# Holding the first four attention chunks to their order of emission, and moving the first weight conversions behind them

## The chip, the cores and the metric

The kernel runs on one core of a Trainium2 chip. The metric is the device time of one execution in microseconds; lower is better. Each comparison ran the kernel before on the same chip in the same rounds. All executions quoted are of the state "fast"; inside that state single executions of one kernel differ by up to 3.3 us (once 5.4 us), and part of this study is about why.

## The reference

The first half is linear attention with a decaying state, for 4 batches, 8 heads, 768 steps and head size 48. The second half is a gated feed-forward network over the 3072 resulting rows of width 384.

```python
f = 1.0 / (1.0 + np.exp(-f_logit))
for t in range(S):
    state = f[:, :, t, :, None] * state + np.einsum('bhd,bhe->bhde', k[:, :, t], v[:, :, t])
    y[:, :, t] = np.einsum('bhd,bhde->bhe', q[:, :, t], state)
...
g = x @ w_gate                     # 384 x 1536
silu = g * (1.0 / (1.0 + np.exp(-g)))
return (silu * (x @ w_val)) @ w_out
```

The weights arrive as 64-bit floats. The kernel turns them into 32-bit floats itself, in 18 pieces of 768 KB.

## The kernel before

The sequence is cut into chunks of 128 steps; a chunk of one batch is one unit of attention (the prediction and the expectations call a unit a chunk). The four units of the first 128 steps (one per batch) come first. From then on the feed-forward matmuls of one group of 128 steps alternate with the attention of the next group. Six steps make up a unit:

```python
def attention(u):                                   # steps 0 to 5, cut
    p = transposed("fTp", fr)                       # TensorE               step 0
    nc.scalar.activation(gate..., p, AF.Sigmoid)    # ScalarE
    yield
    nc.vector.tensor_tensor_scan(tail, gate, ...)   # VectorE, and three small operations   step 1
    yield
    kp = transposed("kTp", kr); qp = transposed("qTp", qr)                # step 2
    nc.vector.tensor_tensor(kT, kp, tail...)        # VectorE
    nc.vector.tensor_tensor_scan(head, gate, start, ...)
    nc.vector.tensor_tensor(qT, qp, head...)
    yield
    # sc <- kT, qT (TensorE); A <- sc * causal (VectorE, two halves); kt       step 3
    yield
    # y <- A, v (TensorE); x <- y (ScalarE); dS <- kt, v; state <- dS          step 4
    yield
    # xTp <- x (TensorE); xT <- xTp (ScalarE)                                  step 5
```

A weight piece takes three calls: a fetch (DMA), `sizes` (two ScalarE operations, `up` and `top`, of some 0.9 us each) and `join` (four VectorE operations, some 3 us together). The order in which the kernel emits all this for the first four units:

```python
for u in range(NRAW): load(u)         # f, k, q, v of three units
keep_warm(5)                          # 5 matmuls of zeros, for the clock of TensorE
...
run(0, 0, 1, 2); load_after(0)
for _ in range(3): fetches.pop(0)()   # three weight pieces
for b in range(1, B):
    if b == 1:
        run(1, 0)
        keep_warm(12)                 # 12 more, in the gap before the first sc
    run(b, 1); run(b - 1, 3); run(b, 2)
    if b + 1 < B:
        run(b + 1, 0)
    else:
        for _ in range(2): sizes.pop(0)()
    run(b - 1, 4)
    if b > 1:
        run(b - 2, 5); load_after(b - 1)
run(B - 1, 3); joins.pop(0)()
run(B - 1, 4); run(B - 2, 5); run(B - 1, 5)
joins.pop(0)(); load_after(B - 1)
```

Emission is not the final order. A scheduler reorders each engine's instructions by its own estimate of when they will be ready. In the build of before it put all 17 warm-up matmuls first, the second unit's scan ahead of the first unit's `kT`, and operations of three weight pieces ahead of the fourth unit's `A`.

## Time and profile before

| | before |
|---|---|
| time, median of the first three executions | 741.44 us |
| span of the profiled execution | 740.4 us |
| first transpose (fTp) / second fTp | 7.39 / 8.70 us |
| first sc / fourth sc | 14.22 / 34.10 us |
| fourth unit's y / first gate matmul | 38.63 / 44.62 us |

The prediction below shows the page, the timeline of TensorE and the chain. In addition, this is the table of windows of the kernel before, in stretches of 10 us: the window and its length, then for each engine the busy time and the number of instructions (matmul, weight load, VectorE, ScalarE, GpSimd), then the granted clock of TensorE, the DMA share and GB/s.

```profile
10.00:20.00 10.00, 5.78 (x35) 5.58 (x35) 7.95 (x15) 0.59 (x2) 0.00 (x0) 0.66 1.02 227
...
30.00:40.00 10.00, 7.30 (x84) 6.11 (x83) 8.37 (x14) 4.93 (x10) 0.00 (x0) 1.00 0.88 200
40.00:50.00 10.00, 9.83 (x33) 6.42 (x33) 4.68 (x8) 4.22 (x8) 0.83 (x1) 0.66 0.44 114
```

Two kinds of loss are to be told apart here. In the first and second line TensorE has too few busy microseconds; in the first and third its clock is 0.66, so a busy microsecond is worth less. The third line looks almost full (9.83) and still loses some 3.3 us (34% of 9.83). A stretch at half clock is called a cold spell below.

### The profile page before, as it was taken

Reading aid. Unit: us, or ns where it says so; the run is one execution under the profiler, and the core shown is the slowest. Engines: PE = TensorE matmul, PEld = TensorE weight load, DVE = VectorE, ACT = ScalarE, POOL = GpSimd, SP = SyncE. Lnnn points to the kernel's source line nnn. Section 1 sums busy time; section 2 is a strip of 40 time slices with the busy share of each in tenths; the row PEclk is TensorE's granted clock in tenths of the full one; section 3 lists DMA queues with packets and bytes.
Section 4 is the critical chain, followed back from the end, with each engine's and each line's share of the span. In section 5 each row is a group of like instructions: output and inputs, shape, how many; then the busy total and the mean of one; then the engine's idle time right before and its main releaser. Section 6 shows DMA issues by size and latency. Waiting matters only on the chain.

```text
span 740.4 us, 7631 instructions
## 1 busy us (share of the span) xinstructions
PE 725.4 (98%) x3146; PEld 420.9 (57%) x3146; DVE 248.5 (34%) x405; ACT 185.0 (25%) x272; POOL 21.0 (3%) x43
## 2 busy tenths in 40 slices
PE   6999999999999999999999999999999999999997
PEld 4855555665565565555566556556555555544454
DVE  6859679303343102423400334310333230011100
ACT  1644566103323012231301322301223120111100
POOL 2000000000000000000000000000000000000000
PEclk8989999999999999999999999999999999999999
DMA  9947556012211101211200121110100000000000
GB/s 185 242 149 190 157 165 171 12 32 43 43 21 33 39 26 34 43 32 33 43 21 23 43 43 22 33 32 22 27 18 1 0 1 22 23 0 1 0 23 24
DMA packets 109772, 38.34 MB, mean 52 GB/s; under 512 B 100512, under 2 KB 103584, under 8 KB 109728
## 3 DMA queue, kind: packets, MB, share of 16 engines
q1 hardware_dynamic: 106272, 33.04, 18.9%
q10 hardware_dynamic: 3456, 4.72, 1.8%
q8 instruction: 27, 0.44, 0.2%
q14 instruction: 17, 0.14, 0.1%
HBM read 33.03 MB, written 4.72 MB: 51 GB/s over the span
## 4 chain that ended last, share of the span: by engine, by line
PE 95%; DVE 3%; ACT 1%; issue 0%; ACTq 0%; DVEq 0%
PE gate L564 25%; PE o L580 25%; PE val L564 25%; PE y L519 5%; PE sc L499 3%; PE y L516 3%; PE kt L506 1%; PE dS L526 1%; PE kTp L462 1%; PE qTp L462 1%; PE fTp L462 1%; PE idle L340 1%; PE xTp L542 1%; DVE tails L472 0%; DVE head L485 0%
## 5 line engine op out<-in xcount | busy, mean ns | idle before, releaser
L564 PE MATMUL gate<-xT,w_gate 128*128 128x512 f32 x432 | 197.7, 599 | 0.8 <-ACT xT L543 0.5
L564 PE MATMUL val<-xT,w_val 128*128 128x512 f32 x432 | 195.7, 595 | 0.1
L580 PE MATMUL o<-w_out,h 128*128 128x384 f32 x576 | 188.8, 487 | 0.0
L580 PEld LDWEIGHTS o<-w_out,h 128*128 128x128 f32 x576 | 108.4, 190 | 73.0 <-issue 0.5
L564 PEld LDWEIGHTS val<-xT,w_val 128*128 128x128 f32 x432 | 79.2, 190 | 86.4 <-issue 85.3
L564 PEld LDWEIGHTS gate<-xT,w_gate 128*128 128x128 f32 x432 | 79.2, 192 | 85.1 <-issue 82.5
L575 DVE TENSOR_TENSOR h<-h,val 128x512 f32<-128x512 f32 x72 | 49.3, 685 | 185.7 <-PE val L564 185.7
L571 ACT ACTIVATE h<-gate 128x512 f32<-128x512 f32 x72 | 43.0, 597 | 208.7 <-PE gate L564 208.5
L472 DVE TENSOR_TENSOR_SCAN tails<-gates,ones 128x516 f32<-128x516 f32 x24 | 29.6, 1233 | 100.2 <-ACT gates L467 100.1
L501 DVE TENSOR_TENSOR A<-sc,causal 128x512 f32<-128x512 f32 x48 | 30.9, 684 | 79.8 <-PE sc L499 79.8
L583 ACT COPY ob<-o 128x384 f32<-128x384 f32 x24 | 11.5, 478 | 183.5 <-PE o L580 183.5
L519 PE MATMUL y<-v,A 128*128 128x48 f32 x384 | 54.4, 270 | 2.7 <-DVE A L501 2.4
L519 PEld LDWEIGHTS y<-v,A 128*128 128x128 f32 x384 | 50.7, 196 | 3.2 <-DVE A L501 2.7
L499 PEld LDWEIGHTS sc<-qT,kT 48*128 48x128 f32 x384 | 24.7, 193 | 20.1 <-issue 17.5
L499 PE MATMUL sc<-qT,kT 48*128 48x128 f32 x384 | 29.7, 292 | 4.9 <-DVE qT L487 4.9
L485 DVE TENSOR_TENSOR_SCAN head<-gates,starts 128x516 f32<-128x516 f32 x24 | 33.7, 1406 | 0.7
L491 POOL TENSOR_TENSOR decayed<-state,tails 128x384 f32<-128x384 f32 x20 | 16.8, 840 | 574.9 <-DVE tails L472 574.9
L516 PE MATMUL y<-decayed,qT 128*128 128x96 f32 x160 | 32.7, 286 | 0.0
L516 PEld LDWEIGHTS y<-decayed,qT 128*128 128x128 f32 x160 | 25.8, 192 | 8.5 <-issue 6.9
L467 ACT ACT_TABLE_LOAD x20 | 25.7, 1283 | 16.1 <-PE fTp L462 13.5
L532 DVE TENSOR_TENSOR state<-decayed,dS 64x192 f32<-64x192 f32 x32 | 11.2, 351 | 48.1 <-PE dS L526 47.9
L571 ACT ACT_TABLE_LOAD x20 | 25.7, 1283 | 0.4
(58 smaller groups left out, 356.1 us busy)
## 6 DMA issues: line engine op xcount, KB each, us to landing
fraw<-in_f_logit_dram SPq DMA_DIRECT2D x24, 192.0 KB, 2.8
kraw<-in_k_dram SPq DMA_DIRECT2D x24, 192.0 KB, 2.7
qraw<-in_q_dram SPq DMA_DIRECT2D x24, 192.0 KB, 3.3
v<-in_v_dram SPq DMA_DIRECT2D x24, 192.0 KB, 3.5
w<-in_moe_w_gate_dram SPq DMA_DIRECT2D x6, 768.0 KB, 5.5
w<-in_moe_w_val_dram SPq DMA_DIRECT2D x6, 768.0 KB, 5.4
w<-in_moe_w_out_dram SPq DMA_DIRECT2D x6, 768.0 KB, 4.3
out_dram<-ob ACTq DMA_DIRECT2D x24, 192.0 KB, 1.8
```

Source lines behind the costliest of these rows:

```text
L462: nc.tensor.transpose(p[:, a * C:(a + 1) * C], src[:, 2 * a:2 * a + 2, :].rearrange("t r d -> t (r d)"), ident)
L467: nc.scalar.activation(pairs(gate)[:, :, 1:N1], p, AF.Sigmoid)
L472: nc.vector.tensor_tensor_scan(tail[:, 0:n][:, ::-1], gate[:, 0:n][:, ::-1], ones[:, ::-1], 1.0, op0=ALU.mult, op1=ALU.add)
L485: nc.vector.tensor_tensor_scan(head, gate[:, 0:n], start, 1.0, op0=ALU.mult, op1=ALU.add)
L499: nc.tensor.matmul(sc[par][:, a * C:(a + 1) * C], lhsT=kT[r, a, :], rhs=qT[r, a, :], start=True, stop=True)
L501: nc.vector.tensor_tensor(A[:, par], sc[par].rearrange("p (a t) -> p a t", t=C), causal.unsqueeze(1).broadcast_to((128, HP, C)), ALU.mult)
L516: nc.tensor.matmul(both, lhsT=qT[:, a, :], rhs=decayed[:, a, :, :].rearrange("p r d -> p (r d)"), start=True, stop=False, skip_group_check ...
L519: nc.tensor.matmul(both[:, par * D:(par + 1) * D], lhsT=A[:, par, a, :], rhs=vt[u][:, 2 * a + par, :], start=(c == 0), stop=True, skip_gro ...
L564: nc.tensor.matmul(p, lhsT=w[:, i, j * 128:(j + 1) * 128], rhs=xT[c][:, i, :], start=(i == 0), stop=(i == KT - 1))
L571: nc.scalar.activation(h[j], p, AF.Silu)
L575: nc.vector.tensor_tensor(h[j], h[j], p, ALU.mult)
L580: nc.tensor.matmul(p, lhsT=h[j][:, b * C:(b + 1) * C], rhs=w_out[:, j, :], start=(j == 0), stop=(j == NF - 1))
```

## The change

Its intent is that TensorE, VectorE and ScalarE run the first four units exactly as emitted: every instruction emitted since a mark gets an order edge (no semaphore, only an order) to the one before it on its engine. The second piece's `sizes` are emitted last, so that they do not stand in ScalarE's way.

```diff
     for u in range(NRAW):
         load(u)
+    traced = nc.cur_bb.bb.instructions
+    mark = traced[-1]
     keep_warm(5)
...
+    def in_order(since):
+        start = next(i for i, ins in enumerate(traced) if ins is since) + 1
+        for engine in (mybir.EngineType.PE, mybir.EngineType.DVE, mybir.EngineType.Activation):
+            mine = [ins for ins in traced[start:] if ins.engine == engine]
+            for a, b in zip(mine, mine[1:]):
+                tc.add_manual_dep(b, a.name, mybir.DependencyInfo(mybir.DependencyClass.NoSync,
+                                                                  mybir.DependencyReason.DATA), reason="order")
...
         else:
-            for _ in range(2):
-                sizes.pop(0)()
+            sizes.pop(0)()
...
     run(B - 1, 5)
+    sizes.pop(0)()
     joins.pop(0)()
     load_after(B - 1)
+    in_order(mark)
```

## The prediction

> **What bounds the kernel now.** I read the page's busy shares and slices first, then the table of windows, then the timeline of TensorE up to 75 us, then the chain of waits through the one hole that is left.
>
> ```profile
> PE 725.4 (98%) x3146; PEld 420.9 (57%) x3146; DVE 248.5 (34%) x405; ACT 185.0 (25%) x272; POOL 21.0 (3%) x43
> ...
> PE   6999999999999999999999999999999999999997
> ...
> PEclk8989999999999999999999999999999999999999
> ```
>
> TensorE is busy for 98% of 740.4 us. Only the first three slices (18.5 us each) show anything else: idle time in the first and third, a lowered clock in the first and third. From about 47 us on TensorE runs without a gap at full clock, so the end is "start of the feed-forward matmuls plus a fixed amount of TensorE work". The change touches only what is before that start: the attention of the first four chunks. In the timeline of TensorE the lines that count are:
>
> ```profile
> 1.25 6.30 PE L340 MATMUL idle<-blank 128*128 128x512 bf16 x17 [1.25 <-DVE blank L335]
> 7.39 0.60 PE L462 MATMUL fTp<-ident,fraw 128*128 128x128 f32 x4
> ...
> 8.70 0.60 PE L462 MATMUL fTp<-ident,fraw 128*128 128x128 f32 x4
> 14.22 2.08 PE L499 MATMUL sc<-qT,kT 48*128 48x128 f32 x16 [4.92 <-DVE qT L487]
> ...
> 38.63 0.42 PE L519 MATMUL y<-v,A 128*128 128x48 f32 x2 [2.41 <-DVE A L501]
> ...
> 44.62 6.62 PE L564 MATMUL gate<-xT,w_gate 128*128 128x512 f32 x12
> ```
>
> All 17 warm-up matmuls run at the very start and delay the first transpose to 7.39, although its data was there at 3.5 (issue at 0.80 plus 2.7 us to landing in the DMA view of that issue). Then TensorE stands idle 4.92 us for VectorE, later 2.41 us more. Each hole brings a cold spell, as the windows show (last three columns: clock, DMA share, GB/s):
>
> ```profile
> 13.50:16.20 2.70, 1.98 (x16) 1.82 (x16) 1.81 (x2) 0.00 (x0) 0.00 (x0) 0.50 1.05 210
> 16.20:19.90 3.70, 3.70 (x20) 3.67 (x18) 2.67 (x4) 0.58 (x1) 0.00 (x0) 0.50 0.99 258
> ...
> 40.50:44.00 3.50, 3.33 (x17) 2.93 (x17) 0.97 (x2) 1.08 (x3) 0.00 (x0) 0.50 0.00 1
> 44.00:47.20 3.20, 3.20 (x8) 1.65 (x7) 1.82 (x5) 2.16 (x3) 0.53 (x1) 0.50 0.50 100
> ```
>
> The second hole comes from conversions of weights that the scheduler put ahead of the last chunk's masking (A). The chain shows it:
>
> ```profile
> 35.73 0.80 ACT top L410
> 36.53 0.02 issue
> 36.55 0.04 DVE top L416
> 36.59 0.44 issue
> 37.03 0.95 DVE top L419
> 37.98 0.61 DVE A L501
> 38.59 0.04 issue
> 38.63 0.42 PE y L519 x2
> ```
>
> VectorE waits for ScalarE's pass over the third weight piece (the timeline gives that wait 1.60 us), and A, whose scores were ready, stands behind it.
>
> **What the Trainium skill says.** "TensorE: Matmul & The Clock Gate", Part 1, says the array runs at half clock until a free-running window of about 3.4 us was busy, and falls back after an idle one. The trace agrees on the size (0.50, two spells of some 6.8 us) and on the cause. By the spacing of the warm-up matmuls, 11 to 12 start in the first 4.3 to 5 us (0.4 us each) and 6 in the last 1.3 us (0.22 us), so the clock came up about 6.2 us after the start, though the page prints full clock there. The same page, in the part on PE-mode transpose, says that transposes do not count as busy for the gate; here the clock came back at 19.9 us after 3.7 us in which TensorE did nothing but transposes, so this trace does not bear it out. Part 1 also says that VectorE and ScalarE take instructions strictly in order, which is what the chain shows at 36.55. "DMA: Bandwidth & Descriptors", Specifications, asks for 512 B or more per descriptor for full rate: the attention loads go in runs of 192 B at about 200 GB/s with a DMA share near 1, the weights' stretch at 18 to 22 us at about 400. So the early loads are bound by the DMA, not by who waits for them, and their landings should stay where they are.
>
> **The change part by part.** By the order of instructions in the two builds:
> 1. Only 5 warm-up matmuls stay at the start. 12 follow the second chunk's fTp, so they lie in the old 4.92 us hole.
> 2. VectorE does each chunk's own chain in turn: the second chunk's scan (1.23 us) no longer precedes the first chunk's qT, and no weight conversion precedes the fourth A.
> 3. The first join follows the fourth A; the second and third pieces' conversions come after the last xT copy.
> 4. From the gate matmuls on the order is nearly as before; five more transposes of chunk five (0.11 us each, 0.55 us) are done before the gate instead of after.
>
> New start S of the first sc: two paths meet. Through VectorE: 5 cold warm-ups end at 3.4; fTp from 3.55, cold, takes 1.06 (as the rows at 17 to 19 us before), to 4.6; sigmoid 0.60, to 5.25; scan 1.23, to 6.5; the three small ones 0.54 (21.85 to 22.39 before); kT 0.6, head 1.15, qT 0.7 with small gaps, to 9.6. Through TensorE: the second chunk's f lands at 7.36 (3.76 + 3.6), fTp to 7.9, 12 warm-ups at 0.216 = 2.6 us, to 10.5. So S = 10.5 if the clock is up by 7.5, instead of 14.22: the warm-ups now cost 0.8 us. If the clock comes up one window later S is about 12; if two, about 13.2.
>
> From S to the first gate, with the warm starts of the rows at 22 to 36 us: sc 1.09, kt 0.49, kTp 0.48, qTp 0.48, fTp 0.44, y 1.81, dS 0.60, xTp 0.48. Chunk 1 without xTp is 5.39, chunk 2 with all 5.87, chunk 3 without fTp 5.43, so the fourth sc is at S + 16.7. It and kt take it to S + 18.3; A ends at S + 18.55 (two of 0.6 us after the second half of sc), so y starts at S + 18.6; y 1.8, dS 0.6, xTp 0.8, fTp 0.45, kTp 0.45, half of qTp 0.2 give S + 22.9. The gate's xT copy ends at about S + 22.7, the first join 2.9 us after A (S + 21.5). VectorE needs 5.4 us a chunk (scan 1.23, small ones 0.54, A 1.2, kT 0.6, head 1.2, qT 0.65), under TensorE's 5.4 to 5.9, so TensorE stays the bound, by 0.5 to 0.7 us.
>
> First gate: 10.5 + 22.9 = 33.4. Before, it was 44.62, and the clock was half until 47.2, which costs (47.2 - 44.62) / 2 = 1.3, so 45.9 in warm time. Saved: 45.9 - 33.4 = 12.5, plus the 0.55 of transposes done earlier = 13.1 us. With the clock one window late 11.6, two late 10.3.
>
> After the gate: w_val's first piece is the tight one. ScalarE starts on it at S + 22.7 and does it and the next one (1.7 us each), VectorE's join follows the other piece's first operation, and ends about 0.4 us before the first val (gate + 5.15). Later pieces land 8 to 18 us after the new gate start, each some 5 us before its matmul. I count nothing for them.
>
> **The rivals.** (a) The warm-ups inside the order become a toll: cold, they cost 0.43 each, 5.1 us, on the path to sc. For it: TensorE idles from 6.35 to 7.4 for the second f, and transposes may count for less. Against: before, the same first five microseconds sufficed. It leaves 10 to 11 us: 731. (b) The weights become the bound, since conversions start later and TensorE asks 12 us earlier. For: the 0.4 us margin, DMA share near 1 until 40 us. Against: only two pieces are needed in the first 10 us and they land by 22.7. It would give back 1 to 4 us: 730 to 733. (c) The strict order itself adds waits, with four PSUM banks turning round; the margins I find are 0.25 to 0.8 us. If VectorE becomes the bound, 0.5 us a chunk: 1 to 2 us. (d) Everything hidden because TensorE has the work to do anyway: no; the saved time is idle time and half clock, which nothing else fills.
>
> **Range and chances.** The best I can build is S = 9.7: 13.9 us saved, 727.5. The middle of the clock cases (6 in 10 early, 3 one window late, 1 two late) is 12.3 us: 741.44 - 12.3 = 729.1; a little friction makes 729.5. Two per cent would need 726.6, which is below my best case, so faster by over 2% takes an error of mine of about 1 us in the favourable direction: 0.1. Within 2%: 0.89. Slower: 0.01. Range 726.8 to 733.5.
>
> **What would show it.** First transpose near 3.6; sc at 10 to 12 with no idle of 4.9 us before it; clock full from about 13 to the end without the 0.50 spells; no wait of y for A above 0.5 us; first gate at 33 to 36; feed-forward busy time per matmul unchanged. I am wrong if the gate starts after 38, if TensorE shows new idle time at val or gate for w_val or w_gate, or if a cold spell lies among the warm-ups or later.

## The result, and the profile after

The changed kernel took 730.33 us (median of 4, 729.28 to 731.38) against 741.32 us for the kernel before. The ratio is 0.9849, with a 95% interval of 0.9829 to 0.9869. Ratios here are the mean time of one kernel's fast runs over that of the other's of the same rounds, so they are not quite the ratio of the medians quoted. That it is faster is beyond doubt, since the interval lies below 1.

The page of the changed kernel, the same lines as before (busy share, busy tenths and clock in 40 slices of 18.2 us):

```profile
PE 718.8 (99%) x3146; PEld 415.8 (57%) x3146; DVE 248.9 (34%) x405; ACT 185.2 (25%) x272; POOL 21.6 (3%) x43
...
PE   8999999999999999999999999999999999999997
...
PEclk9999999999999999999999999999999999999999
```

Only the first slice and the last, which has the same 7 as before, are below 9, and the clock's digit is 9 in all (that is 90% or more; the mean is 0.998). The record does not show the slow start: the five warm-ups took 2.31 us, 0.46 us each, against 0.23 us each for the twelve later ones (2.75 us). The windows in the same stretches:

```profile
10.00:20.00 10.00, 10.00 (x111) 9.02 (x108) 9.37 (x17) 3.47 (x7) 0.00 (x0) 1.00 1.07 249
...
30.00:40.00 10.00, 10.00 (x61) 6.49 (x61) 7.22 (x11) 8.14 (x14) 0.00 (x0) 1.00 1.08 245
40.00:50.00 10.00, 10.00 (x42) 5.03 (x41) 9.93 (x16) 4.24 (x6) 1.39 (x1) 1.00 0.69 189
```

From 10 to 20 us TensorE executes 111 matmuls instead of 35. The timeline of TensorE after the change (start, duration, instruction, and in brackets the idle time before it and what ended that):

```profile
1.25 2.31 PE L340 MATMUL idle<-blank 128*128 128x512 bf16 x5 [1.25 <-DVE blank L335]
3.84 1.09 PE L462 MATMUL fTp<-ident,fraw 128*128 128x128 f32 x4 [0.27 <-POOL state L368]
...
7.41 0.66 PE L462 MATMUL fTp<-ident,fraw 128*128 128x128 f32 x4 [1.06 <-DMA fraw<-in_f_logit_dram]
7.90 2.75 PE L340 MATMUL idle<-blank 128*128 128x512 bf16 x12
10.59 1.16 PE L499 MATMUL sc<-qT,kT 48*128 48x128 f32 x16
...
29.26 0.39 PE L519 MATMUL y<-v,A 128*128 128x48 f32 x2 [0.24 <-issue]
29.81 1.76 PE L519 MATMUL y<-v,A 128*128 128x48 f32 x14 [0.16 <-DVE A L501]
...
33.91 5.36 PE L564 MATMUL gate<-xT,w_gate 128*128 128x512 f32 x12
39.11 5.31 PE L564 MATMUL val<-xT,w_val 128*128 128x512 f32 x12
```

The gap of 4.92 us before the first sc is filled by the 12 warm-ups, and 2.41 us before the fourth y have become 0.24 and 0.16. The wait that remains, 1.06 us, is for the DMA of the second unit's f. The table sets the steps of the prediction beside the two timelines.

| us from the start | before | predicted | after |
|---|---|---|---|
| second fTp | 8.70 | 7.4 | 7.41 |
| first sc | 14.22 | 10.5 | 10.59 |
| fourth sc | 34.10 | 27.2 | 27.28 |
| fourth unit's y | 38.63 | 29.1 | 29.26 |
| first gate | 44.62 | 33.4 | 33.91 |

Where the 12.5 us between the two spans (740.4 and 727.9) come from: 44.62 - 33.91 = 10.7 us before the first gate; half of the 2.58 us from that gate to 47.2, at half clock before, which is 1.3 us; and five transposes done earlier, 0.55 us. The sum is 12.55.

VectorE, behind the fourth A, in the changed kernel:

```profile
28.47 1.29 DVE L501 TENSOR_TENSOR A<-sc,causal 128x512 f32<-128x512 f32 x2 [1.65 <-PE sc L499]
29.68 0.55 DVE L416 TENSOR_SCALAR top<-top 128x768 f32<-128x768 f32 x1
...
37.95 0.95 DVE L420 CUSTOM_DVE_ANT_0 w_val<-top,up 128x1536 uint16<-128x1536 uint16 x1
```

VectorE now waits 1.65 us for TensorE at the fourth A, where before TensorE waited for it. The weights follow. The first `w_val` piece is ready at 38.90 and the first val matmul starts at 39.11, so the margin is 0.2 us.

### The profile page after: what moved, and what is told of

It reads as the page before. It is cut to its first block, busy times and chain, and to the rows that moved or that the text cites. A ratio compares the mean times of both kernels' runs of the same rounds, so it can differ in the third digit from the quotient of the medians.

```text
span 727.9 us, 7635 instructions
## 1 busy us (share of the span) xinstructions
PE 718.8 (99%) x3146; PEld 415.8 (57%) x3146; DVE 248.9 (34%) x405; ACT 185.2 (25%) x272; POOL 21.6 (3%) x43
## 4 chain that ended last, share of the span: by engine, by line
PE 97%; DVE 1%; ACT 1%; DMA 1%; SPq 0%; issue 0%; DVEq 0%
PE o L580 26%; PE val L564 26%; PE gate L564 26%; PE y L519 5%; PE sc L499 4%; PE y L516 3%; PE dS L526 2%; PE kt L506 2%; PE qTp L462 1%; PE kTp L462 1%; PE fTp L462 1%; PE xTp L542 1%; DMA fraw<-in_f_logit_dram 1%; PE idle L340 0%; ACT xT L543 0%; ACT ob L583 0%
## 5 line engine op out<-in xcount | busy, mean ns | idle before, releaser
L485 DVE TENSOR_TENSOR_SCAN head<-gates,starts 128x516 f32<-128x516 f32 x24 | 33.4, 1391 | 0.6
```

The source lines that it names most:

```text
L485: nc.vector.tensor_tensor_scan(head, gate[:, 0:n], start, 1.0, op0=ALU.mult, op1=ALU.add)
```

## The experiments

The theory has two sources of gain that are worth separating: (1) the 12 warm-ups leave the head of the path and fill the hole before the first sc, so that the clock stays full there; (2) VectorE finishes each unit's chain before it starts on the next or on weights. Rival A says only the warm-ups matter, rival B only VectorE's order. The edges of ScalarE were not tested apart from those of VectorE. All kernels gave correct results. Diffs are against the changed kernel.

**Edges on TensorE only.**

```diff
-        for engine in (mybir.EngineType.PE, mybir.EngineType.DVE, mybir.EngineType.Activation):
+        for engine in (mybir.EngineType.PE,):
```

> Order edges on TensorE only; VectorE and ScalarE are scheduled freely. The built order: 5 warm-ups, then 12 behind the second fTp, but the second chunk's scan again ahead of the first chunk's head, and the first operations on weights ahead of the fourth A. My theory (the gain has two sources, warm-ups out of the way and in the hole, and VectorE's order): first sc at about 12 instead of 10.6, because the second scan waits for its sigmoid; no cold spell near 13 us; 732 to 735 us, some two thirds of the gain. Rival A (only the warm-ups matter): 730. Rival B (only VectorE's order matters): 738 to 741.

Measured: 735.48 us median, ratio 0.9928 (0.9891 to 0.9965). The four executions fall into two groups: 732.59 and 733.46 with a mean clock of 1.0 and 0.999, and 737.49 and 738.00 with a clock of 0.99 in both. The median lies just above the range that I gave (732 to 735). The profile is of the first group; no execution of the second was profiled. TensorE's and ScalarE's timelines:

```profile
12.38 1.16 PE L499 MATMUL sc<-qT,kT 48*128 48x128 f32 x16 [1.38 <-DVE starts L477]
...
26.92 0.66 PE L462 MATMUL qTp<-ident,qraw 128*128 128x128 f32 x4 [1.07 <-DVE A L501]
...
33.04 1.76 PE L519 MATMUL y<-v,A 128*128 128x48 f32 x14 [0.16 <-DVE A L501]
```

```profile
21.40 0.90 ACT L408 ACTIVATE up<-w 128x768 int32<-128x768 uint32 x1 [1.31 <-DMA w<-in_moe_w_gate_dram]
22.20 0.58 ACT L467 ACTIVATE gates<-fTp 128x512 f32<-128x512 f32 x1
```

The first sc came at 12.38, as the theory said. A hole that I had not expected is the one at 26.92: ScalarE took up a weight piece that had not landed, the fourth unit's sigmoid stood behind it, and the wait passed on to the scan, to A (with another 0.53 us for a weight operation right ahead of that A) and from there to TensorE's qTp, most likely through a PSUM bank, a buffer for TensorE's results. The old hole before the fourth y, on the other hand, was gone without any edge on VectorE, since the scheduler here put no weight operation that had to wait right ahead of A. So that hole belongs to one schedule and does not come about in each schedule without edges.

**Edges on VectorE and ScalarE only.**

```diff
-        for engine in (mybir.EngineType.PE, mybir.EngineType.DVE, mybir.EngineType.Activation):
+        for engine in (mybir.EngineType.DVE, mybir.EngineType.Activation):
```

> Order edges on VectorE and ScalarE only; TensorE is free, and all 17 warm-ups are at the start again. My theory: first fTp near 7.4, first sc near 13.1, TensorE idle about 3.8 us before it, so a cold spell of 6.8 us follows in most phases of the clock's window (3 us lost), but no hole before the fourth chunk's y and no second cold spell; first gate at 38 to 40, 733 to 736 us. Rival A (only the warm-ups matter): 740. Rival B (only VectorE's order matters): 730.

Measured: 736.48 us median (735.57 to 736.93, just above the range of 733 to 736 that I gave), ratio 0.9937 (0.9920 to 0.9953). The timeline of TensorE and two windows:

```profile
12.11 2.08 PE L499 MATMUL sc<-qT,kT 48*128 48x128 f32 x16 [3.65 <-DVE qT L487]
```

```profile
11.30:14.60 3.30, 2.49 (x18) 2.29 (x19) 2.57 (x6) 0.00 (x0) 0.00 (x0) 0.50 1.08 211
14.70:18.00 3.30, 3.30 (x18) 3.30 (x16) 2.69 (x4) 0.70 (x2) 0.00 (x0) 0.50 1.03 204
```

With the warm-ups in front again, the hole before sc is 3.65 us and a cold spell follows; the first gate starts at 38.47. About 0.9 us of the earlier start in this profile is not the edges' doing: its 17 warm-ups took 5.37 us, against 6.30 us in the profile of the kernel before.

Both rivals fall. The order of VectorE and ScalarE alone is worth about 5 us (741.46 - 736.48). TensorE's order alone, which is mostly the place of the warm-ups, is worth 8.4 us in the group with the full clock (741.46 less the mean of that group) and 3.7 us in the other. Over all four executions it is worth some 6 us, and 5 and 6 add up to the 11 to 12 us that both bring together. Whether the two gains overlap cannot be told from this.

**The late weights alone, without edges.**

```diff
-    in_order(mark)
```

> No order edges; only the emission of the second weight piece's sizes is moved behind the last xT copy. The scheduler gives almost the order of before on all three engines (17 warm-ups first, conversions still ahead of the fourth A). My theory: 741 us, same as before within 1 us, with both holes and both cold spells. Rival (the late weights are what removes the hole before the fourth y): that hole is gone, 735 to 737.

Measured: 741.88 us, ratio 1.0004 (0.9987 to 1.0020). Both holes are where they were:

```profile
14.43 2.08 PE L499 MATMUL sc<-qT,kT 48*128 48x128 f32 x16 [4.93 <-DVE qT L487]
...
38.88 0.42 PE L519 MATMUL y<-v,A 128*128 128x48 f32 x2 [2.41 <-DVE A L501]
```

Moving this emission did nothing while the scheduler was free to move it back.

**All edges, the second piece's sizes early as before.**

```diff
         else:
-            sizes.pop(0)()
+            for _ in range(2):
+                sizes.pop(0)()
...
     run(B - 1, 5)
-    sizes.pop(0)()
     joins.pop(0)()
```

> All order edges, but the second weight piece's sizes stay where before has them, ahead of the third chunk's x copy on ScalarE. My theory: x of the third chunk comes 1.2 us later, which holds PSUM banks and delays the fourth sc or kt by 0.5 to 1 us; w_val is ready some 2 us earlier than needed; 730.5 to 731.5 us. Rival A (moving the weights behind is worth much): 733 or more. Rival B (w_val's margin is the bound after the change, so early sizes help): 729 or less.

Measured: 729.84 us (729.64 to 731.05), ratio 0.9850, no difference from the changed kernel that four executions can show. The delay that I expected is there, in the fourth sc, which takes 1.72 us instead of 1.16:

```profile
27.16 1.72 PE L499 MATMUL sc<-qT,kT 48*128 48x128 f32 x16
```

The first gate starts at 34.15 against 33.91. The delay was foreseen, but the median lies 0.7 us below the range that I gave (730.5 to 731.5): its effect on the time is less than can be told here. Both rivals (733 or more, 729 or less) fall, and this part of the change is worth next to nothing.

**24 warm-ups instead of 12.**

```diff
-            keep_warm(12)
+            keep_warm(24)
```

> The changed kernel with 24 instead of 12 warm-up matmuls behind the second fTp. My theory (from the first sc to the end TensorE is the bound, so every microsecond put in front of the first sc is paid in full): first sc at 13.2 instead of 10.6, first gate at 36.5, 12 times 0.216 = 2.6 us more than the changed kernel: 732.5 to 733.5. Rival (VectorE or the weights bind somewhere after the first sc and give slack): less than half of it comes through, 730 to 731.5.

Measured: 733.78 us (733.69 to 735.32), ratio 0.9904. The first sc is at 13.16 and the first gate at 36.47, 2.57 and 2.56 us later than in the changed kernel, as the 2.6 expected. The span grew by 4.2 us, however (732.1 against 727.9), and the median lies 0.3 us above the range that I gave. The rest lies after the gate:

```profile
51.27 1.16 PE L499 MATMUL sc<-qT,kT 48*128 48x128 f32 x16 [1.49 <-DVE qT L487]
```

The build had moved the fifth unit's qT on VectorE behind more weight operations, outside the stretch that the edges cover. So delay before the first sc is paid in full, as the theory has it, and in the unprotected stretch behind a changed schedule cost another 1.5 us.

**No warm-ups in the gap, and 8 of them.**

```diff
-            keep_warm(12)
+            keep_warm(8)        # or the line left out
```

> The changed kernel without the 12 warm-up matmuls behind the second fTp; 5 stay at the start. The first sc is then bound by VectorE, at 9.7 to 9.9 instead of 10.6, with TensorE idle some 1 us before the second fTp and 1.8 us after it. My theory (the warm-ups fill the hole for the clock's sake): in many executions the clock falls or does not come up in time, a half-clock stretch of some 7 us costs up to 3.5 us, and the times spread: median 730.5 to 734, some executions near 729.5. Rival (such short holes do not matter to the clock): 729.5 in all, 0.8 us better than the changed kernel.

> The changed kernel with 8 instead of 12 warm-up matmuls behind the second fTp. They end at 9.6, just before qT is there. My theory: first sc at 9.75 instead of 10.6, clock still full, 0.8 us off: 729 to 730, at the edge of what 5 rounds can tell. Rival (the four fewer let the clock fall): 731 or more.

Measured: 730.36 us (730.28 to 731.28) without, 730.28 us (728.74 to 730.45) with 8; ratios 0.9851 and 0.9841. Without warm-ups sc came at 9.73 as expected, and then the clock was half (the windows of that kernel):

```profile
5.20:8.60 3.40, 1.60 (x11) 0.98 (x10) 3.19 (x6) 0.61 (x2) 0.00 (x0) 1.00 1.06 208
8.70:15.40 6.70, 5.67 (x34) 5.48 (x34) 5.29 (x10) 0.59 (x2) 0.00 (x0) 0.50 1.11 219
```

That execution (731.28) reached the first gate at 35.68, 1.8 us later than the changed kernel, although its sc was 0.86 us earlier: there the cold spell took back more than the shorter path brought. It is the slowest of the five; the other four lost less (730.3). Unlike what I expected, the times hardly spread, and the median lies just below the range I gave; the mean clock was 0.995 to 0.997 in all five executions, against 0.997 or 0.998 in the first four executions of the changed kernel and 0.999 in four of the five later ones. With 8 warm-ups there were two groups: 728.74 and 729.04 at a clock of 1.0 and 0.999, and three at 730.3 to 730.5 at 0.997. The median lies 0.3 us above the range that I gave. The profile is of the second group. It has the first sc at 11.54 and not at 9.75, and shows a clock that fell at about 7.8, just after the 1.33 us hole before the second fTp, and came back:

```profile
4.45:7.80 3.35, 1.68 (x12) 1.10 (x11) 2.98 (x10) 0.60 (x1) 0.41 (x2) 1.00 1.06 210
7.90:11.20 3.30, 3.30 (x11) 1.31 (x9) 3.09 (x6) 0.60 (x1) 0.00 (x0) 0.50 1.13 223
```

The 8 warm-ups took 3.40 us at half clock, where the changed kernel's 12 took 2.75. So the warm-ups in the gap act on the clock; that the phase of the clock's window decides which execution is hit is likely and not shown.

What they are worth is little. Without any of them the median was 730.36 us, with 12 it was 730.33 us and 729.66 us (two submissions), so by the medians filling the hole brings at most 0.7 us and perhaps nothing. Of the first source, then, nearly all lies in taking the 12 out of the front of the path, and little in putting them into the hole.

**The second unit's f loaded earlier.** The remaining hole waits for that load, and the 12 warm-ups stand behind it.

```diff
-    for u in range(NRAW):
-        load(u)
+    for u, parts in ((0, "fkq"), (1, "f"), (0, "v"), (1, "kqv"), (2, "fkqv")):
+        load(u, parts)           # load() issues only the parts named
```

> The changed kernel with the second chunk's f loaded ahead of the first chunk's v, 12 warm-ups kept. f then lands about 1 us earlier (6.4), the second fTp follows qTp without the 1 us wait, the warm-ups end near 9.5, and sc starts with qT at 9.7 to 9.9: 0.8 us off, 729 to 730, with no hole for the clock, so no slow executions. Rival (the load that is moved is not what the warm-ups wait for, or v is late for y): 730.5 or more.

Measured: 728.78 us (728.65 to 730.65), ratio 0.9830. Four of five lie between 728.65 and 728.84. The profile happened to be of the fifth (730.65), where sc came at 10.02 and a cold spell fell on the end of the four units (windows):

```profile
27.80:31.20 3.40, 3.01 (x31) 2.62 (x30) 3.24 (x5) 0.70 (x2) 0.00 (x0) 1.00 1.04 203
31.30:34.60 3.30, 3.30 (x26) 3.21 (x22) 0.93 (x1) 2.67 (x7) 0.00 (x0) 0.50 1.04 203
```

That there would be no slow executions was wrong, then.

**The three side by side on one chip, and two more warm-ups at the fourth y.** The third kernel is the one with the early f and this line:

```diff
     run(B - 1, 3)
+    keep_warm(2)
     joins.pop(0)()
```

> The changed kernel, unedited, five rounds on the chip of the two kernels below. In its first four executions it had two at 729.3 to 729.7 and two at 731.0 to 731.4, and the page of one of the fast ones shows no cold spell. My theory (the phase of the clock's window decides between none and one cold spell of 3.4 us, worth up to 1.7 us): two groups again, 729.3 to 729.7 and 730.8 to 731.4, median between them. Rival (the spread is ordinary noise): one group around 730.3.

> The kernel with the second chunk's f loaded ahead of the first chunk's v, again, beside the changed kernel on one chip. My theory: most executions at 728.6 to 728.9, a few at 730.5 where a cold spell of 3.4 us falls on the fourth chunk's y (as in its first profile, at 31.2 us); mean 1 to 1.5 us below the changed kernel. Rival (it was luck of phases): within 0.5 us of the changed kernel's mean.

> The same with 2 more warm-up matmuls behind the fourth chunk's kt, where TensorE waits 0.24 and 0.16 us for A and then runs the slow y. They take 0.43 us and cost 0.1 to 0.3 us. My theory (the holes around y let the window count as idle): no execution at 730.5 any more, all at 728.7 to 729.0. Rival (y itself, 48 columns a matmul, counts as idle, holes or not): the slow executions stay, and all others are 0.2 us worse.

Measured, five executions each, beside nine of the kernel before (median 741.51):

| | executions, us | mean |
|---|---|---|
| changed kernel | 729.36, 729.61, 729.66, 729.86, 731.15 | 729.93 |
| f earlier | 728.87, 728.93, 729.01, 730.52, 730.69 | 729.60 |
| f earlier, 2 warm-ups at y | 728.83, 728.91, 729.19, 729.25, 729.25 | 729.09 |

Over both submissions the changed kernel had 3 of 9 executions at 731.0 to 731.4 and the other 6 at 729.3 to 729.9; with f earlier 3 of 10 were at 730.5 to 730.7 and 7 at 728.65 to 729.01. So the typical execution gains 0.7 us from the early f, near the 0.8 first expected, and the slow group stays. The means side by side differ by 0.33 us only, not by the 1 to 1.5 us that I expected of them. That is the figure of the rival (within 0.5 us), so a gain in the mean is not shown. In the third kernel no execution was slow. With 3 slow in 10 for the second kernel, five in a row without one would come about by chance in 0.7 to the fifth power, 17%, of cases, so this is a hint that holes around y make the spell, and not proof. This kernel has the best mean, 0.8 us below the changed kernel on the same chip, and a ratio of 0.9832 (0.9817 to 0.9847) to the kernel before. The intervals of the other two, 0.9844 (0.9827 to 0.9861) and 0.9841 (0.9824 to 0.9859), overlap with it, so that it beats them is not shown.

## Why the prediction was right

It said 729.5 (726.8 to 733.5) and 730.33 was measured, 729.66 in five later executions.

- **The bound.** That the end is the first gate plus a fixed amount of TensorE work held: the three terms of the sum before the gate, at the gate and for the transposes give 12.55 of the 12.5 us of the span.
- **The first sc.** Predicted at 10.5 through the load of f and the warm-ups, measured 10.59. The load landed at 7.37 (7.36 predicted). That the warm-ups cost 0.8 us on the path is confirmed from both sides: with 24 of them sc is later by 2.57 us, with none it is at 9.73.
- **From sc to the gate.** Predicted 22.9, measured 23.3. The fourth sc came at S + 16.7 in both. The term that was mis-sized is the end of the fourth A, and with it "y 1.8". The prediction had A done at S + 18.55, before y starts; it ended at 29.76, S + 19.17, since both halves (1.29 us) came after the last sc. Two matmuls of y ran at 29.26, the other 14 waited for A, and from y's first matmul to dS 2.24 us passed (29.26 to 31.50).
- **The cold spells.** Both are gone in the profile, as predicted. The step about the clock had a size that fits (0, 1.5 or 2.8 us; the fast and slow groups are 1.6 to 1.8 us apart) but named only a late rise before the first sc, which no trace of this kernel shows. That 6 in 10 were given to the early clock and 6 of 9 executions were fast is luck, then. In all the traces with 12 warm-ups in the gap they ran at full clock, in 2.75 to 2.78 us. The spell that a trace caught is at the fourth y, in the kernel with the early f. For the changed kernel itself no slow execution was profiled, so whether its slow group is that spell or the one that the 8 warm-ups showed before sc stays open.
- **Rival (a), the toll of cold warm-ups,** was seen only with 8 of them, 3.40 us. **Rival (b), weights as the bound,** did not come about, but the margin at the first val was 0.2 us and not 0.4. **Rival (c), waits from the strict order,** amounts to the 0.4 us at y, of which the 0.24 us before y's first matmul were in the sum already (kt at S + 18.3, y at S + 18.6). VectorE had less slack than the 0.5 to 0.7 us a unit that I gave it: it waited 0.39 us for the first sc, not at all for the second and 0.35 us for the third. The 1.65 us at the fourth come from there being no scan of a next unit ahead of that A.
- **Three readings of the record.** The page shows no idle time in the third slice (its digit is 9); the table of windows and the timeline do. And the clock came back at 19.9 us after 3.5 us of transposes (16.24 to 19.70) and 0.2 us of y, not after 3.7 us of transposes alone. And that the trace agrees with a window of 3.4 us "on the cause" was too strong: the second cold spell followed a hole of 2.41 us.
- **The late weights.** I gave them no gain of their own; alone they give none (741.88), and left out they cost nothing that can be told (729.84).

## What to carry to other kernels

When one engine is busy 98% of the time, look at the stretch that is not: a start-up of 45 us held 12.5 us here. The slow clock behind a hole can cost as much as the hole: before, 4.92 us of idle time were followed by 5.68 us of work at half clock, a loss of some 2.8 us, and 2.41 us by 6.53 us of such work, some 3.3 us. The order in the source need not be the order on the engine; read the built order, and pin it where a chain is tight, on every engine that takes part, since a free one moved the hole elsewhere. A filler in front of the path is paid in full (12 more of them moved the first sc by 2.57 us). In the hole it brought at most 0.7 us here by the medians, so try it against leaving it out.

## What the Trainium skill lacked or had wrong

- "TensorE: Matmul & The Clock Gate", the part on PE-mode transpose, says that transposes do not count as busy for the clock. In the kernel before the clock came back at 19.9 us after 3.5 us of nothing but transposes and 0.2 us of y, and with edges on VectorE and ScalarE only it was back in the window from 18.1 us on, after 3.5 us of them (14.13 to 17.60) and 0.5 us of y. But busy time of this kind did not always suffice: before, the window from 40.5 to 44.0 us was busy for 3.33 us with y and then transposes, and half clock went on to 47.2. That these transposes (`nc.tensor.transpose`, MATMUL in the trace) use the mode that the page means is taken for granted.
- The same page, "Why this matters for your kernels", warns of idle gaps above about 3 us; neither that row nor what the page says of short idles between groups of matmuls gives a size for smaller ones. In the kernel before a gap of 2.41 us was followed by half clock from 40.4 us on. Elsewhere a window with 1.68 of 3.35 us busy (8 warm-ups) and one with 3.01 of 3.40 us busy, most of it narrow y matmuls of 48 columns, were each followed by half clock of some 3.4 us. Windows of nearly the same work in other executions were not (in the changed kernel y ran at 29.26 to 31.50 and the clock stayed full), so this is no threshold.
- The same page, Part 1, puts the penalty of the ramp to full clock below 1% of a typical span and advises not to fit to a count of cold matmuls. The differences between groups here are below 1% too (1.6 to 1.8 us of 730), but for comparing two versions of one kernel they matter: edges on TensorE only gave 733 us at a mean clock of 1.0 and 738 us at 0.99, so several executions and the mean clock of each are wanted before such a difference is believed.
